# A fused RWKV-7 and SiLU feed-forward kernel: the same 1437 steps in another written order, with other PSUM places

## The chip, the cores and the metric

The kernel runs on one core of one Trainium2 chip. The metric is the device time of one execution in microseconds, from the first to the last instruction and what lies around them; the time before is the median of three runs. TensorE is called PE in the profile (PEld is its weight load), VectorE is DVE, ScalarE is ACT, GpSimd is POOL and SyncE is SP.

## The reference

An RWKV-7 recurrence over 768 tokens for 4 batches and 8 heads of 40 channels, and behind it a feed-forward layer with SiLU on its output, all in float32.

```python
for t in range(S):                                   # S = 768, state is (B, H, D, D), D = 40
    y[:, :, t] = np.einsum('bhd,bhde->bhe', rt, state)
    Sa = np.einsum('bhde,bhe->bhd', state, at)
    state_decay = state * wt[:, :, None, :] - np.einsum('bhd,bhe->bhde', Sa, bt)
    state = state_decay + np.einsum('bhd,bhe->bhde', vt, kt)
...
x = attn_out.transpose(0, 2, 1, 3).reshape(B * S, H * D)   # 3072 x 320
h = x @ w_in                                         # 320 x 2048
g = h * (1.0 / (1.0 + np.exp(-h)))
out = g @ w_out                                      # 2048 x 320
```

## The kernel before

The 768 tokens are cut into 12 chunks of 64 (`NN` = 12). Inside a chunk the recurrence is turned into small matrix products and one triangular inverse per head and batch, 32 of them; from chunk to chunk goes the state `G`. What a chunk does, by the functions that make its steps and the lines that the profile shows for them:

- `load`, `load_r`: SP issues the DMAs of w, b, a, k (512 KB each), v, r and the transposed v.
- `prepare`: DVE makes the running products of w by two scans (`down` L473, `up` L491), scales b and k (`aside`, L510) and a (`scale`, L500). PE multiplies them (`between`, L528, once for b and once for k), DVE masks the k product (L577), PE multiplies it by v (`sv`, L592) and turns k and b (`turn`, L617); ACT copies the results out of PSUM.
- `special` (chunks 0 to 2) and `inverse`/`merge` (the rest, two chunks at a time): the triangular inverse. DVE does it in many small `dots` (L643 multiply, L644 reduce). For chunk 0 PE brings the blocks into place (`spread` L720) and back (`gather` L778). In `special`, `both` (L833), a turn (L846) and three rounds of `more` (L890, added up by DVE in L909) finish it; in `merge`, `first` (L975) and `second` (L1004).
- `chain`: the recurrence from chunk to chunk. PE `right` (L1046, reads `G`), DVE adds it (L1056), PE `solve` (L1070) and `solve_t` (L1101), ACT and DVE copy these out (`vu`, `vut`), PE turns `G` (L1131) and does `update` (L1158), DVE adds to and scales `G` (L1174).
- `read`: PE `look` twice (L1204), DVE masks each (L1216, into `lam`), PE `write_state` (L1243) and `write` (L1258), DVE scales (L1269); the result goes through DRAM into `xt` (`bring`; for chunk 0 straight to `xt`, L1313).
- `moe`: the feed-forward layer of the 256 tokens of the chunk. PE `full` (L1340, 8 matmuls of 128x256) and `rest` (L1353), ACT SiLU (`gate`, L1363), PE `second` (L1380, in pieces of 4 matmuls of 128x320, eight pieces a chunk), then a copy and two stores.
- `weights`: once, the layer's weights come as 64-bit floats through POOL's DMAs and are made into float32 by DVE and ACT (L336 to L354); for three of the ten units PE adds two halves (`sum_`, L360, 128x512) and DVE multiplies (L372).

Every call of `add` makes one step; each step has an engine and a PE shape: `F` is the full 128x128 array (`full`, `second`, `sum_`), `R` 64 rows by 128 columns (`rest`), `H` 128 rows by 64 columns or less (`update`, `write`), `Q` 64x64 quarters (most of the recurrence), `T` the turns, `S` 32x32 (`first`, `second` of `merge`). Nothing sorts the steps when the kernel is built: `Plan.follow` takes them in the order of the numbers in the table `ORDER` and gives each PSUM or `lam` buffer the place that its digit in `SLOTS` names. Each engine carries out its own steps in that order, one after another, and waits at a step for what it reads, for what still reads the place that it writes, and for nothing else. PSUM is four places, `pair0` to `pair3`, of 4 KB in each partition; two `lam` buffers are in SBUF. DMAs stand in the queue of SP, ACT or POOL in the same order, and a DMA that waits holds up those behind it on its queue.

The lines of this that the change works through:

```python
        for room, slot in zip(rooms.values(), slots):
            room.slot, room.tile = int(slot), self.slots[room.kind][int(slot)]
...
        return [self.ops[n] for n in order]
...
        for op in plan.follow([int(n) for n in ORDER.split()], "".join(SLOTS.split())):
            op["do"]()
```

Of the kernel before, what the change touches and what calls it, by code (L numbers as in the profile page):

```python
# [130 lines left out]
"""  # L131

SLOTS = """
02010313103013023201121220321321331102201331232212021000300010012010102103230113332111021202013323111302020230
10211001211003132011132330130003220300213021120013103110133031021231131031100212001201232130132032033001101332
32011022330030001301001320110132012332222001102003101210203231232113030320232121101130100132012
"""
# [1471 lines left out]
```

## Time and profile before

| | |
|---|---|
| median of 3 runs | 690.67 us (689.32 to 693.51) |
| span of the profiled execution, first to last instruction | 690.3 us |
| last matmul ends | 684.3 us |
| DVE busy | 420.9 us, 61% of the span |
| ACT busy | 198.4 us, 29% |
| POOL busy | 13.0 us, 2% |

The profiled execution's own time is its span, and the median of the runs is 0.4 us above it. A matmul in float32 stands in the trace as two records, so that a piece of `second` is 8 records and a `full` 16. Matmul records overlap, since the array is a pipeline; what a step takes on PE is therefore read from its start to the start of the next one and not from its own length. A row of the timeline gives start, length, engine, line, operation and tiles, the number of records, and in brackets the idle time in front with what ended it.

### The profile page before, as it was taken

The page shows a single profiled execution, that of the slowest core. Times are in us where ns is not written, and L with a number is a line of the kernel's source. Part 1 is how long each engine was busy: PE and PEld are TensorE (multiplying, and loading weights), DVE is VectorE, ACT ScalarE, POOL GpSimd, SP SyncE. Part 2 cuts the span into 40 slices and gives each one's busy share as a digit, 9 for nine tenths or more (in the row PEclk, how much of TensorE's full clock was granted, in tenths as well). Part 3 has the DMA queues.
Part 4 walks back from the last instruction along what each step waited for, and adds up shares of the span by engine and source line. Part 5 has one row for each costly group of instructions (what it writes and reads, how often), then busy time and mean ns, then how long its engine had stood idle before and what let it go on. Part 6 is the DMA issues. An engine that isn't in the chain of part 4 may idle for free.

```text
span 690.3 us, 27487 instructions
## 1 busy us (share of the span) xinstructions
PE 656.6 (95%) x12794; PEld 531.4 (77%) x12794; DVE 420.9 (61%) x632; ACT 198.4 (29%) x254; POOL 13.0 (2%) x30
## 2 busy tenths in 40 slices
PE   1589999999999999999999999999999999999996
PEld 1467788788778778878778778778788778788774
DVE  7998988984894558954538962639854773011000
ACT  4562364343214332214222222222223122121020
POOL 3000110000000000000000000000000000000000
PEclk9999999999999999999999999999999999999999
DMA  9945385725255462561730672352542214111100
GB/s 291 296 125 138 92 257 168 183 37 133 78 140 120 103 167 63 128 159 27 194 103 14 193 166 66 104 134 74 152 86 65 74 35 105 28 45 34 42 2 22
DMA packets 113282, 76.64 MB, mean 111 GB/s; under 512 B 61154, under 2 KB 109589, under 8 KB 112520
## 3 DMA queue, kind: packets, MB, share of 16 engines
q1 hardware_dynamic: 110436, 63.71, 36.0%
q0 software_dynamic: 2224, 10.63, 4.7%
q8 instruction: 102, 1.67, 1.0%
q10 hardware_dynamic: 500, 0.46, 0.3%
q14 instruction: 20, 0.16, 0.1%
HBM read 60.03 MB, written 14.35 MB: 108 GB/s over the span
## 4 chain that ended last, share of the span: by engine, by line
PE 87%; DVE 7%; DMA 2%; issue 1%; SPq 1%; ACT 1%; POOL 1%; DVEq 0%; ACTq 0%; POOLq 0%
PE pair L1380 31%; PE pair L1340 24%; PE pair L1353 7%; PE pair L1204 4%; PE pair L528 3%; PE pair L1258 3%; PE pair L1158 2%; PE pair L617 2%; PE pair L1046 2%; PE pair L592 2%; PE pair L1243 2%; PE pair L1070 1%; PE pair L1101 1%; PE pair L890 1%; DVE kbv L473 1%
## 5 line engine op out<-in xcount | busy, mean ns | idle before, releaser
L1380 PE MATMUL pair<-wo,gts 128*128 128x320 f32 x768 | 215.8, 437 | 0.0
L1380 PEld LDWEIGHTS pair<-wo,gts 128*128 128x128 f32 x768 | 143.4, 190 | 58.0 <-issue 1.0
L1340 PE MATMUL pair<-xt,wi 128*128 128x256 f32 x768 | 175.8, 383 | 0.0
L1340 PEld LDWEIGHTS pair<-xt,wi 128*128 128x128 f32 x768 | 143.5, 190 | 22.1 <-issue 0.7
L1363 ACT ACTIVATE gts<-pair 128x1024 f32<-128x1024 f32 x48 | 47.6, 1026 | 91.2 <-PE pair L1353 84.1
L644 DVE TENSOR_REDUCE XI<-XI 128x64 f32<-128x512 f32 (+9 forms) x85 | 58.7, 690 | 2.9
L1216 DVE TENSOR_TENSOR lam<-pair,ml 128x1024 f32<-128x1024 f32 x22 | 26.4, 1220 | 46.6 <-PE pair L1204 29.4
L1353 PE MATMUL pair<-xt,wi 64*128 64x256 f32 x384 | 48.0, 389 | 0.8 <-DMA xt<-X 0.8
L261 DVE COPY ot<-pair 128x320 f32<-128x320 f32 x22 | 10.8, 489 | 57.0 <-PE pair L1380 49.4
L528 PE MATMUL pair<-a,kb 40*64 40x64 f32 x1536 | 30.1, 228 | 15.0 <-DVE a L500 13.4
L1353 PEld LDWEIGHTS pair<-xt,wi 64*128 64x128 f32 x384 | 35.3, 187 | 7.1 <-issue 2.0
L528 PEld LDWEIGHTS pair<-a,kb 40*64 40x64 f32 x1536 | 26.9, 141 | 17.2 <-issue 15.0
L643 DVE TENSOR_TENSOR XI<-XI,mi 128x1024 f32<-128x1024 f32 (+8 forms) x60 | 33.6, 560 | 5.1 <-DMA mi<-md 3.8
L510 DVE TENSOR_TENSOR kb<-kbv 128x512 f32<-128x512 f32 (+1 forms) x36 | 29.9, 862 | 6.6 <-PE pair L528 3.3
L630 ACT COPY kt<-pair 128x640 f32<-128x640 f32 x24 | 16.5, 695 | 56.1 <-PE pair L617 55.9
L1204 PEld LDWEIGHTS pair<-r,vut 40*64 40x64 f32 x1536 | 24.4, 135 | 5.2 <-issue 2.8
L473 DVE TENSOR_TENSOR_SCAN kbv<-wz,zt 128x1024 f32<-128x1024 f32 x12 | 27.5, 2292 | 0.6
L1204 PE MATMUL pair<-r,vut 40*64 40x64 f32 x1536 | 26.8, 220 | 1.0 <-DMA r<-in_rT 0.9
L491 DVE TENSOR_TENSOR_SCAN wz<-wz,zt 128x1024 f32<-128x1024 f32 x12 | 27.5, 2289 | 0.3
L259 ACT ACTIVATE vut<-pair 128x1024 f32<-128x1024 f32 (+1 forms) x13 | 12.5, 958 | 49.4 <-PE pair L1101 45.4
L643 DVE TENSOR_TENSOR XI<-XI,xs 128x1024 f32<-128x1024 f32 (+1 forms) x25 | 25.2, 1008 | 0.6
L937 ACT COPY mi<-XI 128x1024 f32<-128x1024 f32 x5 | 10.0, 2002 | 51.8 <-DVE XI L644 31.7
(160 smaller groups left out, 685.2 us busy)
## 6 DMA issues: line engine op xcount, KB each, us to landing
wz<-in_wT SPq DMA_DIRECT2D x12, 512.0 KB
a<-in_aT SPq DMA_DIRECT2D x12, 512.0 KB
kbv<-in_bT SPq DMA_DIRECT2D x12, 512.0 KB
kbv<-in_kT SPq DMA_DIRECT2D x12, 512.0 KB
vut<-in_vT SPq DMA_DIRECT2D x48, 96.0 KB
r<-in_rT SPq DMA_DIRECT2D x48, 96.0 KB
vu<-in_v SPq DMA_DIRECT2D x24, 160.0 KB
xh<-lam SPq DMA_DIRECT2D x22, 160.0 KB
```

The costliest lines, as they stand in the source:

```text
L473: nc.vector.tensor_tensor_scan(back(V), back(W[:, 2 : 2 + Q * C]), zt, 1.0, ALU.mult, ALU.add)
L491: nc.vector.tensor_tensor_scan(Z, Z, zt, 0.0, ALU.mult, ALU.add)
L510: TTn[engine].tensor_tensor(out=at_(kb, place(is_b, first), (576 * step, 4 // step), (128, 4), (1, C)), in0=blocks((kf, bf)[is_b]), in1=bl ...
L528: nc.tensor.matmul(room.tile[half(b), j, g * C : g * C + C], lhsT=kb[rows(j), place(is_b, q) : place(is_b, q) + C], rhs=A[rows(j), q * C : ...
L643: nc.vector.tensor_tensor(out=at_(tmp, 0, *dims), in0=x, in1=y, op=ALU.mult)
L644: nc.vector.tensor_reduce(out=out_, in_=at_(tmp, 0, *dims), axis=AX.X, op=ALU.add)
L1204: nc.tensor.matmul(pl.tile[half(1 - b if role else b), b, c * C : c * C + C], lhsT=vut[rows(b), role, hu, :], rhs=rs[rows(b), hh, :], star ...
L1216: lambda pl=pl, la=la: nc.vector.tensor_tensor(out=la.tile.rearrange("p (q t) -> p q t", q=Q), in0=pl.tile.rearrange("p a b -> p (a b)").r ...
L1340: nc.tensor.matmul(rooms[g].tile[:, f // 2, (f % 2) * T : (f % 2) * T + T], lhsT=wi[:, k, (4 * g + f) * 128 : (4 * g + f) * 128 + 128], rh ...
L1353: nc.tensor.matmul(rooms[g].tile[:, h, (f % 2) * T : (f % 2) * T + T], lhsT=wi3[half(h), g * 256 + (f % 2) * 128 : g * 256 + (f % 2) * 128 ...
L1363: nc.scalar.activation(out=gts[:, 4 * g * T : 4 * g * T + 4 * T], in_=rooms[g].tile.rearrange("p a b -> p (a b)"), func=AF.Silu)
L1380: nc.tensor.matmul(po[b].tile[:, 0, 0:DM], lhsT=g4[:, f, 128 * b : 128 * b + 128], rhs=wo[:, f, :], start=f == 0, stop=f == NF - 1,)
```

## The change

The change exchanges the two tables `ORDER` and `SLOTS` and nothing else. The same 1437 steps (417 on SP, 394 on DVE, 386 on PE, 223 on ACT, 17 on POOL) stand in another order from the first step on, on every engine, and the buffers have other PSUM and `lam` places. Counted along PE's steps, the shape changes from one to the next 224 times before and 149 times now. Of these, 139 and 64 lie between the full array (`F`) and another shape; the other 85 and 85 lie among the smaller shapes. Up to the first `second` (L1380) PE does the same steps in both orders, but for two that now stand ahead of it, an `sv` of chunk 2 and the `update` of chunk 1; the changes of shape there are 43 before and 40 now, of which 29 and 17 at the full array. From there on they are 181 and 109, of which 110 and 47 at the full array.

```diff
@@ -72,68 +72,68 @@
 ORDER = """
-102 24 0 147 2 114 1 3 4 70 67 6 7 8 9 10 103 14 104 105 15 148 25 106 149 11 115 139 127 150 73 66 75 151 16
...
+24 102 0 1 3 2 70 6 7 9 8 114 127 115 103 104 11 12 13 10 105 106 76 77 78 67 75 74 69 71 5 68 287 64 4 72 14
...
 SLOTS = """
-02010313103013023201121220321321331102201331232212021000300010012010102103230113332111021202013323111302020230
...
+01011322123213010132113203302101221020123002030101100100023213112021212323111122102121120001002203113101021013
...
```

On DVE the first place is the start of the program, behind the `down` scan of chunk 0 (`a_82` is a of chunk 0, `wz_73` and `wz_74` the w of chunks 0 and 1, `kb` the scaled k and b; L336 to L345 belong to the weights):

```order
 L488 MEMSET wz_73 128x16
+L510 TENSOR_TENSOR kb<-kbv 128x2x4x64 x2
 L491 SCALAR_TENSOR_TENSOR wz_73<-wz_73,zt 128x1024
 L492 MEMSET zt 128x16
-L510 TENSOR_TENSOR kb<-kbv 128x2x4x64 x2
+L336 TENSOR_SCALAR wi<-gts 128x2x512
+L510 TENSOR_TENSOR kb<-kbv 128x4x4x64
 L500 TENSOR_TENSOR a_82<-a_82,wz_73 128x1024
-L336 TENSOR_SCALAR wi<-gts 128x2x512
```

The scaling of a, which PE's first step needs, now has one weight step and the scaling of k ahead of it. Behind it, up to the three instructions of L733 that begin the inverse of chunk 0, DVE had ten instructions of weights, masks and the scaling of k; now it has two of the weights (L338, L339) and the whole `down`, `between_` and `up` of chunk 1, which stood behind that inverse before.

On PE at the same place, from the first matmul on, before (`sb_88` is the b product of chunk 0 in SBUF, `XI` holds the blocks of its inverse, `gts` the raw weights):

```order
L528 MATMUL pair_111<-a_82,kb 64x64 x32
L720 MATMUL pair_112<-ident,sb_88 64x64 x32
L528 MATMUL pair_113<-a_82,kb 64x64 x32
L617 MATMUL pair_114<-ident,kb 128x40 x16
L617 MATMUL pair_111<-ident,kb 128x40 x16
L360 MATMUL pair_113<-gts,ident 128x512
L778 MATMUL pair_114<-ident,XI 64x64 x32
```

and now:

```order
L528 MATMUL pair_111<-a_82,kb 64x64 x32
L617 MATMUL pair_112<-ident,kb 128x40 x16
L720 MATMUL pair_113<-ident,sb_88 64x64 x32
L617 MATMUL pair_114<-ident,kb 128x40 x16
L360 MATMUL pair_111<-gts,ident 128x512 x3
L528 MATMUL pair_112<-a_82,kb 64x64 x32
L360 MATMUL pair_111<-gts,ident 128x512
L778 MATMUL pair_113<-ident,XI 64x64 x32
```

Three more weight sums stand ahead of `gather` (L778), and one turn ahead of `spread` (L720).

In the middle of the program, PE in chunk 2's `chain` and `read`, from `solve_t` (L1101) on, before:

```order
L1101 MATMUL pair_113<-X_93,R_92 40x64 x32
L1380 MATMUL pair_111<-wo,gts 128x320 x4
L1204 MATMUL pair_113<-r,vut 64x64 x32
L592 MATMUL pair_112<-vu_99,lam_116 64x40 x32
L1380 MATMUL pair_111<-wo,gts 128x320 x4
L1204 MATMUL pair_112<-r,vut 64x64 x32
L1243 MATMUL pair_113<-r,GT 40x64 x32
L1380 MATMUL pair_111<-wo,gts 128x320 x4
L617 MATMUL pair_114<-ident,kb 128x40 x16
```

and now:

```order
L1101 MATMUL pair_113<-X_93,R_92 40x64 x32
L592 MATMUL pair_112<-vu_99,lam_116 64x40 x32
L1070 MATMUL pair_111<-R_92,X_93 64x40 x32
L1204 MATMUL pair_113<-r,vut 64x64 x32
L1204 MATMUL pair_112<-r,vut 64x64 x32
L1243 MATMUL pair_111<-r,GT 40x64 x32
L1158 MATMUL pair_113<-vu_98,kt_87 40x40 x32
L1258 MATMUL pair_111<-lam_116,kt_87 40x64 x16
L1258 MATMUL pair_111<-lam_115,kt_87 40x64 x16
L617 MATMUL pair_112<-ident,kb 128x40 x16
L1380 MATMUL pair_114<-wo,gts 128x320 x16
```

The pieces of `second` that stood between the small steps now follow as one block of 16 matmuls (four pieces). The same is done in most chunks. Between the second `look` and `write` there was a piece of `second` or a `full` before in most chunks; now there are `write_state` and `update`, or `first` and `update`.

DVE's order at this place of chunk 9, now: the two masks of `look` (L1216) directly one behind the other, the state's sum behind them (`vu_99` is that chunk's v and u):

```order
L263 TENSOR_SCALAR vu_99<-pair_111 64x2x4x80
L1216 TENSOR_TENSOR lam_115<-pair_113,ml 128x1024
L1216 TENSOR_TENSOR lam_116<-pair_114,ml 128x1024
L1174 TENSOR_TENSOR G<-pair_113,G 128x2x8x40
L261 COPY ZQ<-pair_111 32x512
L1174 TENSOR_TENSOR G<-G,wc_108 128x2x8x40
L1269 TENSOR_TENSOR lam_115<-pair_112,wz_73 128x4x4x64
```

What moved there is work of the inverse (L643, L644), of which before some stood ahead of the masks and more between the masks and the sum; now it starts behind these rows.

On SP, w, b, k, a of chunk 0 is now the order of the first four loads (w, a, b, k before). On POOL, the fetch of the last unit of `w_in` went from the second to the sixth place, and POOL's four of the DMAs that bring chunk 0's result into `xt` (L1313) stand ahead of all fetches of `w_out` but one. The last step of all is now the count of the finite checks (L1448 to L1459), whose matmul ran at 549.6 us before.

More of the change, by code (lines that the diff above doesn't have):

```diff
@@ L74 @@
 ORDER = """
[56 rows of a table removed]
[56 rows of a table added]
 """
 SLOTS = """
-02010313103013023201121220321321331102201331232212021000300010012010102103230113332111021202013323111302020230
-10211001211003132011132330130003220300213021120013103110133031021231131031100212001201232130132032033001101332
-32011022330030001301001320110132012332222001102003101210203231232113030320232121101130100132012
+01011322123213010132113203302101221020123002030101100100023213112021212323111122102121120001002203113101021013
+01302021033120123011331300011303032122211212203212312000130232321031100212210310003323331103131011100031202031
+20301020121121001301021033021103222302323120101230303111330203022112010120101323201021302301230
 """
```

110 rows, old and new, of the table ORDER are left out of this document.

## The prediction

> **What bounds the kernel now.** I read the page first, then PE's waits, then the span in stretches.
>
> ```profile
> span 690.3 us, 27487 instructions
> PE 656.6 (95%) x12794; PEld 531.4 (77%) x12794; DVE 420.9 (61%) x632; ACT 198.4 (29%) x254; POOL 13.0 (2%) x30
> ```
>
> Two answers follow: who PE waited for (in total, times, longest), and busy time by stretch (us, PE, PEld, DVE, ACT, POOL, granted clock, DMA share, GB/s).
>
> ```profile
> PE pair L528 <- DVE a L500: 13.4, 1, 13.4
> PE pair L778 <- ACT XI L773: 6.7, 1, 6.7
> ```
>
> ```profile
> 0.00:13.30 13.30, 0.00 (x0) 0.00 (x0) 10.24 (x32) 5.14 (x5) 6.62 (x19) 1.00 0.87 300
> 0.00:117.00 117.00, 90.10 (x2248) 73.58 (x2248) 103.56 (x172) 54.17 (x65) 11.87 (x28) 0.97 0.66 193
> 33.50:60.00 26.50, 24.03 (x604) 18.53 (x604) 24.90 (x37) 12.70 (x17) 0.57 (x1) 0.94 0.50 137
> 117.00:684.40 567.40, 566.52 (x10548) 457.77 (x10546) 317.38 (x461) 143.85 (x190) 1.12 (x2) 1.00 0.37 95
> ```
>
> There are two kernels in one. From 117 us, where the first L1380 starts, PE works 566.5 of 567.4 us: what it does there, it pays in full, and nothing else counts as long as it is never kept waiting. Before 117 us PE is idle 26.9 us (117.0 less 90.1), 13.4 of them ahead of its first matmul and 13.5 in waits, while DVE works 103.6: that part is a chain through DVE with PE in it. The change touches both, so the sum has a term for each.
>
> **Term 1, the changes of shape.** The same instructions cost PE more or less by what stands beside them. Start times say it best (rows of the timeline: start, length, operation, records).
>
> ```profile
> 605.04 3.62 PE L1340 MATMUL pair<-xt,wi 128*128 128x256 f32 x16
> 608.49 2.32 PE L1380 MATMUL pair<-wo,gts 128*128 128x320 f32 x8
> 610.64 3.62 PE L1340 MATMUL pair<-xt,wi 128*128 128x256 f32 x16
> 614.19 1.10 PE L1101 MATMUL pair<-X,R 64*40 64x64 f32 x64
> ```
>
> ```profile
> 173.57 1.16 PE L1204 MATMUL pair<-r,vut 40*64 40x64 f32 x64
> 174.55 1.09 PE L592 MATMUL pair<-vu,lam 64*64 64x40 f32 x64
> 175.57 2.42 PE L1380 MATMUL pair<-wo,gts 128*128 128x320 f32 x8
> 177.92 1.16 PE L1204 MATMUL pair<-r,vut 40*64 40x64 f32 x64
> ```
>
> Between two full-array steps an L1380 takes 610.64 - 608.49 = 2.15 us; between two small ones 177.92 - 175.57 = 2.35. So 0.10 for each of its two boundaries. A full L1340 takes 3.45 ahead of another full step and 614.19 - 610.64 = 3.55 ahead of a small one: 0.10 again. The small neighbour pays too: L1204 took 0.98 ahead of L592, and L592 took 1.02 ahead of L1380, while the L592 at 301.26 (quoted below) took 0.95 ahead of a small step: 0.07. A stay in the full array so costs 0.20 on its own side and about 0.07 on the side of the step before it, 0.27 for two boundaries, or 0.14 each. Bounds: 0.10 if the small side saves nothing, 0.20 if it pays as much as the full side at both of its ends.
>
> The order has 75 boundaries of the full array fewer (139 to 64); the changes among the smaller shapes stay 85. 75 x 0.14 = 10.5 us, bounds 7.5 and 15.0; I take the value that is measured on both sides. 63 of them lie behind the first L1380, where PE is the bound, so they count in full; the other 12 are in PE's part of the start. The Trainium skill says in TensorEngine Tiling (Array Packing), Key Properties, that a change of the tiling mode, not of the tile alone, drains the array. By that rule every change of shape would cost, so that only the 75 fewer of 224 are saved, which is what the rows give too; the page has no price, and the rows have one.
>
> **Term 2, the start.** The chain of chunk 0 in DVE's and PE's rows:
>
> ```profile
> 12.09 1.22 DVE L500 TENSOR_TENSOR a<-a,wz 128x1024 f32<-128x1024 f32 x1
> 13.22 0.69 DVE L336 TENSOR_SCALAR wi<-gts 128x1024 int32<-128x1024 int32 x1
> 24.52 1.51 DVE L733 SCALAR_TENSOR_TENSOR xs<-pair,dm,xs 128x256 f32<-128x256 f32 x3
> 32.23 0.23 DVE L471 TENSOR_SCALAR w<-wz,pad 128x16 f32<-128x16 f32 x1
> 38.24 1.20 DVE L791 TENSOR_TENSOR mi<-pair,dm 128x1024 f32<-128x1024 f32 x1
> ```
>
> ```profile
> 13.41 1.99 PE L528 MATMUL pair<-a,kb 40*64 40x64 f32 x64 [13.41 <-DVE a L500]
> 16.68 3.65 PE L720 MATMUL pair<-ident,sb 64*64 64x64 f32 x61 [1.29 <-ACT sb L259]
> 24.72 2.07 PE L360 MATMUL pair<-gts,ident 128*128 128x512 f32 x2
> 33.50 3.75 PE L778 MATMUL pair<-ident,XI 64*64 64x64 f32 x64 [6.71 <-ACT XI L773]
> 37.18 1.17 PE L360 MATMUL pair<-gts,ident 128*128 128x512 f32 x2
> ```
>
> The first matmul waits for L500, and now one L336 (0.7) and the second L510 (as large as L500, which took 13.22 - 12.09 = 1.13 to the next start) stand ahead of it: 13.4 + 1.8 = 15.2. The loads should be there: with a, the fourth on SP now, 2 MB have come there, beside 1 or 2 MB of weights on POOL, and the first 13.3 us moved 300 GB/s, 4 MB. That is just in time, and a late by 1 us is the bound above.
>
> L720 started 3.27 behind the first matmul. From 15.2, it can start at 18.5 and end at 22.1, and ACT's copy of it takes 0.5: 22.6. DVE comes to L733 behind L338 and L339 (1.1 and 0.6, as L500 and L336) and the scans of chunk 1, which took 38.24 - 32.23 = 6.0: a's scaling ends at 15.2, so at 22.9. L733 starts at 22.9 instead of 24.5, and `gather` (L778) is asked for at 33.5 - 1.6 = 31.9. Behind it the scans no longer hold up L791.
>
> PE has three more weight sums and one L528 ahead of `gather`. The sums wait for ACT's two conversions of the raw weights:
>
> ```profile
> 21.64 0.47 ACT L750 ACTIVATE xs<-pair,dm 128x256 f32<-128x256 f32 x1
> 23.04 1.22 ACT L340 ACTIVATE gts<-gts 128x1024 f32<-128x1024 int32 x1
> 24.12 0.70 ACT L630 COPY kt<-pair 128x640 f32<-128x640 f32 x1
> 24.70 1.16 ACT L354 ACTIVATE gts<-gts 128x1024 f32<-128x1024 uint32 x1
> ```
>
> Behind L750 at 22.6 come L630 and these two, 0.6 + 1.1 + 1.1, so the first sum at 25.3, some 2.5 us after PE's last turn. Four sums of 1.1 (37.18's kind) and an L528 of 1.0 fill PE to 30.7, and `gather` waits 1.2 instead of 6.7. At half speed (24.72's sum took 2.07) they end at 35.6 and `gather` is 2.1 us late instead of 1.6 early. Waits now: 0.4 ahead of L720 (18.5 less 15.2, the matmul's 2.0 and a turn of 0.9), 2.5, 1.2, and of the others (13.5 less 6.7 ahead of L778 and the 1.3 between 15.4 and L720's 16.68, so 5.5) I keep 2, since those behind `gather` hang on L791, which the scans held up: 6.1 in place of 13.5. So +1.8 and -7.4: -5.6. Bounds: 0 (the waits fall by 1.8 alone) and -9 (the 2 and part of the 2.5 vanish).
>
> DVE doesn't forbid it. Before, its last step for the first L1380, the weights' product, was
>
> ```profile
> 105.47 1.22 DVE L352 TENSOR_TENSOR wo<-wo,raw 128x1024 f32<-128x1024 f32 x1
> ```
>
> done at 106.7, 10.4 us ahead of PE. Now four instructions more stand ahead of it, one of L336's size and three of L500's, 4.3 us: 111.0 with all its old idle time. PE comes at 117.1 - 5.6 + 2.3 (the two steps more) - 1.7 (12 boundaries of Term 1): 112.1.
>
> The stretch from 33.5 to 60 shows the granted clock at 0.94, and the sum at 24.72 ran at half the speed of the one at 37.18. The Trainium skill (TensorE: Matmul & The Clock Gate, What's actually happening) has half the clock by default and after an idle window of about 3.4 us: by it the sums ahead of `gather` start at half speed, and the start saves up to 3.7 us less (35.6 for 31.9). The rows agree that it was slow there, but not for how long PE must work first: 24.72 comes after 8 us of nearly unbroken matmuls.
>
> **Term 3, new waits behind 117 us.** Small steps now follow each other without a `second` between them, so their copies must fit under less.
>
> ```profile
> L1216 DVE TENSOR_TENSOR lam<-pair,ml 128x1024 f32<-128x1024 f32 x22 | 26.4, 1220 | 46.6 <-PE pair L1204 29.4 <-issue 9.5 <-ACT kt L630 7.6
> ```
>
> ```profile
> 281.42 1.40 PE L1158 MATMUL pair<-vu,kt 128*40 128x40 f32 x64
> 282.74 1.16 PE L528 MATMUL pair<-a,kb 40*64 40x64 f32 x64
> ...
> 301.26 1.14 PE L592 MATMUL pair<-vu,lam 64*64 64x40 f32 x64
> 302.21 1.12 PE L1046 MATMUL pair<-G,a 40*64 40x40 f32 x64
> 303.26 0.75 PE L975 MATMUL pair<-ZQ,sb 32*32 32x32 f32 x64
> 303.95 3.72 PE L1340 MATMUL pair<-xt,wi 128*128 128x256 f32 x16
> ```
>
> Between the second `look` and `write` stand `first` (303.95 - 303.26 = 0.69) and `update` (1.32), 2.0 us, or `write_state` and `update`, 2.3. Under them one mask of 1.22 must end, begun about 0.2 late behind the first mask: 1.4 us. It fits with 0.6 to spare, because the masks stand next to each other. Before, all waits behind 117 us were 0.9 together (567.4 less 566.5); I take 1.2 more, 0.1 in each of eleven chunks, with bounds 0 and 6 (0.5 in each).
>
> The rest costs nothing: POOL's fetch of the last `w_in` unit, moved behind four others, is needed by the fourth L1340 alone, just ahead of the first L1380; of SP's queue the four loads of chunk 0 stay first; `xt` of chunk 0 goes ahead of the fetches of `w_out` on POOL, and the check's matmul at the end runs beside the last copy and store, which end the span.
>
> **Sum.** 690.3 - 10.5 - 5.6 + 1.2 = 675.4 on the profile's own span; the median is 0.4 above it: 675.8.
>
> **The rivals.** *The start gives nothing* (waits move, clock low): 690.7 - 10.5 + 1.2 = 681.4. For it: the half-speed sums, and `gather`'s chain with every later step behind it. Against it: DVE ends L352 10 us before PE needs it, so there is room.
>
> *A new wait in every chunk, and slower.* If the three instructions from L471 to the scan behind it, or another 2.3 us of DVE's work (a scan is near half of the 6.0 above), get between `look`'s product and its mask, `write` waits 2.3 + 1.4 - 2.0 = 1.7 us, and `right` behind the state's sum once more, some 3 us a chunk in eleven chunks: 690.7 - 16.1 + 33 = 708. It takes the gain away at 14.9 / 11 = 1.4 us a chunk and is slower by 1% from 2.0. Against it stands DVE's order at that place, masks next to each other.
>
> *The boundary's price belongs to the step and not to the change* (what a stay saves at its edge comes back inside the longer run, as waits for the PSUM places that a run needs at once): 690.7 - 5.6 + 1.2 = 686.3, within 1%. Against it: runs of L1380 inside the full array are 2.15 in every row of that kind.
>
> **How the numbers follow.** One per cent, about what a measurement of this kernel can tell from no change, is 6.9 us: faster means below 683.8. The forecast has 0.72; the start that gives nothing 0.15; the price that comes back 0.08; the wait in every chunk 0.05. Faster 0.87, same 0.08, slower 0.05. Below, Term 1 at 15.0 or the start at -9 take off 4.5 or 3.4, and both hardly come together: 668. Above, the start at 0 gives the first rival's 681.4, and 1.6 more of Term 3 on it 683. What lies outside is the 0.13 of the last two rivals and some 0.05 below: 668 to 683.
>
> **What would show it.** After its start PE is busy all but a microsecond or two from the first L1380 on; an L1380 takes 2.15 inside its run and no row of 2.35 but at single pieces; the first matmul is at 15.2, `gather` near 32, the first L1380 between 107 and 114. Wrong it is if PE's waits list names L1216, L1174 or L1363 with more than 5 us together, or if the first L1380 is behind 117.

## The result: 12.7% slower, and the profile after

The changed kernel takes 780.37 us (775.76 to 782.41, four runs), the one before 690.56 beside it: a ratio of 1.127, interval 1.122 to 1.132. The forecast was 675.8. Ratios here and below leave out executions more than 1.5% above the fastest of the same kernel, where the granted clock is lower too.

The profile's first lines, its instruction queue (packets, MB, share of 16 DMA engines), and two stretches, to the first L1380 and from there to the last matmul:

```profile
span 779.6 us, 27470 instructions
PE 692.2 (89%) x12794; PEld 574.0 (74%) x12794; DVE 422.0 (54%) x632; ACT 197.3 (25%) x254; POOL 12.5 (2%) x30
...
q8 instruction: 102, 1.67, 0.9%
```

```profile
0.00:132.50 132.50, 90.76 (x2376) 76.11 (x2376) 99.83 (x164) 54.77 (x67) 11.36 (x28) 0.94 0.59 171
132.60:772.60 640.00, 601.38 (x10426) 497.82 (x10418) 321.93 (x467) 142.12 (x188) 1.12 (x2) 0.92 0.32 84
```

The same 12794 matmuls now keep PE busy 692.2 us instead of 656.6. On the profiled spans (779.6 against 690.3) the 89.3 us divide so: the first L1380 starts at 132.6 instead of 117.1, 15.5 us; from there to the end of the last matmul 640.0 instead of 567.2, 72.8; behind it 1.0. In that middle part PE is idle 640.0 - 601.4 = 38.6 us (0.9 before) and busy 34.9 us longer, though it has fewer boundaries; the granted clock is 0.92 there and was 1.00. The records of the clock show two values only, full and half, and 99 us of the 640 at half.

PE's waits in the middle part (total, times, longest):

```profile
PE pair L592 <- issue: 8.3, 4, 2.8
PE pair L1204 <- issue: 7.8, 6, 1.8
PE pair L1243 <- issue: 5.1, 4, 2.0
PE pair L528 <- issue: 4.1, 3, 1.5
PE pair L1070 <- issue: 4.0, 4, 1.4
...
PE pair L1204 <- DMA mi<-md: 1.5, 1, 1.5
```

Hardly anything is waited for: "issue" is time in which the engine waited for nothing that the profile shows. With the rows left out it comes to 36.0 us, all of it ahead of small steps. No mask and no state sum is in the list; two copies of ACT's and the SiLU (L1363) are, with 1.0 us together. Where it happens, in chunk 4 behind a run of eight L1380:

```profile
278.67 1.14 PE L1046 MATMUL pair<-G,a 40*64 40x40 f32 x64
279.62 1.70 PE L528 MATMUL pair<-a,kb 40*64 40x64 f32 x99
282.82 1.00 PE L528 MATMUL pair<-a,kb 40*64 40x64 f32 x27 [1.50 <-issue]
283.54 0.32 PE L1101 MATMUL pair<-X,R 64*40 64x64 f32 x2
...
288.35 0.77 PE L1204 MATMUL pair<-r,vut 40*64 40x64 f32 x32
290.64 1.56 PE L1204 MATMUL pair<-r,vut 40*64 40x64 f32 x91 [1.52 <-DMA mi<-md]
...
292.05 0.66 PE L1243 MATMUL pair<-r,GT 40*40 40x64 f32 x33
294.09 1.09 PE L1243 MATMUL pair<-r,GT 40*40 40x64 f32 x30 [1.38 <-issue]
295.11 2.36 PE L1158 MATMUL pair<-vu,kt 128*40 128x40 f32 x64
297.26 3.23 PE L1258 MATMUL pair<-lam,kt 128*40 128x64 f32 x64
300.43 0.92 PE L1340 MATMUL pair<-xt,wi 128*128 128x256 f32 x3
```

The gaps stand in the middle of steps, not at their starts, where a step would wait for its operands. L1158 and L1258 behind the last gap take 297.26 - 295.11 = 2.15 and 3.17 us; L1158 took 1.32 before. The records of the clock have it at half from 293.1 to 299.9.

What the gaps have in common comes out of the trace by counting. Number PE's instructions (matmuls, weight loads and PE's own waits on semaphores) from the start, and set the packets of the instruction queue beside them, each 1.67 MB / 102 = 16.4 KB:

```
gap ends   gap    PE's instruction,   the last packet of the
(us)       (us)   modulo 256          instruction queue ended
242.48     2.84   194                 1.64 us earlier
282.82     1.50   193                 1.34
290.64     1.52   194                 0.91
294.09     1.38   194                 1.34
353.49     2.73   194                 1.37
397.43     1.79   193                 1.50
401.15     1.61   193                 1.34
```

Of the 29 gaps above 0.35 us behind 117 us, 28 end at instruction 193 or 194 modulo 256, 0.9 to 1.6 us behind the end of an instruction packet. So PE gets its instructions 256 at a time and had come to the end of what was there; the gap at 290.64 is one of them too, put down to a DMA by the rule that the last event is to blame. The number 193 itself says nothing, since the trace doesn't show what PE ran ahead of its first recorded instruction; that it is the same each time does. No two packets start less than 3.41 us apart in this trace, and 3.10 in that of before. A small step is 128 such instructions in 0.95 us, two of them use a packet up in 1.9; an L1380 is 16 instructions in 2.15. The Trainium skill has the size (Advanced Engine Details and Errata, ISA Cache: lines of 256 instructions, and only two of them, though it gives TensorE four times the memory of the others); the trace agrees by the count of 256, and the blocks below, which stall after 332 to 524 instructions, fit two lines. How long a line takes to come that section doesn't say.

### The profile page after: what moved, and what is told of

Its sections match the earlier page's. It is cut to its first block, busy times and chain, and to the rows that moved or that the text cites. A ratio compares the mean times of both kernels' runs of the same rounds, so it can differ in the third digit from the quotient of the medians.

```text
span 779.6 us, 27470 instructions
## 1 busy us (share of the span) xinstructions
PE 692.2 (89%) x12794; PEld 574.0 (74%) x12794; DVE 422.0 (54%) x632; ACT 197.3 (25%) x254; POOL 12.5 (2%) x30
## 3 DMA queue, kind: packets, MB, share of 16 engines
q8 instruction: 102, 1.67, 0.9%
## 4 chain that ended last, share of the span: by engine, by line
PE 85%; issue 6%; DMA 5%; DVE 2%; SPq 1%; ACT 1%; DVEq 0%; ACTq 0%
PE pair L1380 27%; PE pair L1340 22%; PE pair L1353 6%; PE pair L1204 4%; PE pair L1258 4%; DMA wz<-in_wT 3%; PE pair L528 3%; PE pair L1158 3%; PE pair L890 2%; PE pair L1243 2%; PE pair L1101 2%; PE pair L592 2%; PE pair L1070 2%; PE pair L617 2%; PE pair L1046 2%
## 5 line engine op out<-in xcount | busy, mean ns | idle before, releaser
L1380 PE MATMUL pair<-wo,gts 128*128 128x320 f32 x768 | 215.3, 440 | 0.0
L1380 PEld LDWEIGHTS pair<-wo,gts 128*128 128x128 f32 x768 | 146.6, 193 | 61.3 <-issue 3.4
L1340 PE MATMUL pair<-xt,wi 128*128 128x256 f32 x768 | 170.7, 381 | 0.0
L1340 PEld LDWEIGHTS pair<-xt,wi 128*128 128x128 f32 x768 | 145.4, 190 | 21.3
L1363 ACT ACTIVATE gts<-pair 128x1024 f32<-128x1024 f32 x48 | 47.1, 1024 | 201.6 <-PE pair L1353 201.4
L644 DVE TENSOR_REDUCE XI<-XI 128x64 f32<-128x512 f32 (+9 forms) x85 | 58.7, 690 | 2.9
L528 PE MATMUL pair<-a,kb 40*64 40x64 f32 x1536 | 32.2, 231 | 29.4 <-DVE a L500 22.9
L528 PEld LDWEIGHTS pair<-a,kb 40*64 40x64 f32 x1536 | 28.5, 144 | 31.6 <-issue 31.1
L1204 PE MATMUL pair<-r,vut 40*64 40x64 f32 x1536 | 36.6, 257 | 11.9 <-issue 10.4
L1353 PE MATMUL pair<-xt,wi 64*128 64x256 f32 x384 | 46.3, 386 | 0.0
L1216 DVE TENSOR_TENSOR lam<-pair,ml 128x1024 f32<-128x1024 f32 x22 | 26.6, 1222 | 32.4 <-PE pair L1204 31.0
L1204 PEld LDWEIGHTS pair<-r,vut 40*64 40x64 f32 x1536 | 33.9, 169 | 13.6 <-issue 11.9
L643 DVE TENSOR_TENSOR XI<-XI,mi 128x1024 f32<-128x1024 f32 (+8 forms) x60 | 33.7, 562 | 10.8 <-DMA mi<-md 9.2
L263 DVE TENSOR_SCALAR vu<-pair 64x640 f32<-64x640 f32 x9 | 7.3, 817 | 50.8 <-ACT vu L259 50.8
L1258 PE MATMUL pair<-lam,kt 128*40 128x64 f32 x704 | 29.5, 259 | 0.2 <-issue 0.2
L1258 PEld LDWEIGHTS pair<-lam,kt 128*40 128x40 f32 x704 | 28.0, 149 | 1.1 <-issue 1.0
L1269 DVE TENSOR_TENSOR lam<-pair,wz 128x1024 f32<-128x1024 f32 x11 | 13.5, 1223 | 23.3 <-PE pair L1258 23.3
```

The source lines that it names most:

```text
L528: nc.tensor.matmul(room.tile[half(b), j, g * C : g * C + C], lhsT=kb[rows(j), place(is_b, q) : place(is_b, q) + C], rhs=A[rows(j), q * C : ...
L643: nc.vector.tensor_tensor(out=at_(tmp, 0, *dims), in0=x, in1=y, op=ALU.mult)
L644: nc.vector.tensor_reduce(out=out_, in_=at_(tmp, 0, *dims), axis=AX.X, op=ALU.add)
L1204: nc.tensor.matmul(pl.tile[half(1 - b if role else b), b, c * C : c * C + C], lhsT=vut[rows(b), role, hu, :], rhs=rs[rows(b), hh, :], star ...
L1258: nc.tensor.matmul(py.tile[rows(j), b, c * C : c * C + C], lhsT=K[:, q, j], rhs=lam[m].tile[:, l * C : l * C + C], start=fresh(py, b, j), ...
L1340: nc.tensor.matmul(rooms[g].tile[:, f // 2, (f % 2) * T : (f % 2) * T + T], lhsT=wi[:, k, (4 * g + f) * 128 : (4 * g + f) * 128 + 128], rh ...
```

## The experiments

**The two halves.** One kernel has the changed order up to its first L1380 and the rest in the order of before, one the reverse; PSUM places follow in a few buffers. Of ORDER's rows in the first:

```diff
-102 24 0 147 2 114 1 3 4 70 67 6 7 8 9 10 103 14 104 105 15 148 25 106 149 11 115 139 127 150 73 66 75 151 16
+24 102 0 1 3 2 70 6 7 9 8 114 127 115 103 104 11 12 13 10 105 106 76 77 78 67 75 74 69 71 5 68 287 64 4 72 14
...
```

> The changed order up to its first L1380, then the rest of the steps in the order of before, with PSUM places to suit. Theory S (supply): PE's instructions come in packets of 256 on the instruction queue, no packet sooner than about 3.5 us after the last; small steps use one up in 1.9 us, and only pieces of the full array between them give the queue time. Theory C (clock): unbroken small tiles alone bring the granted clock down, and the gaps only follow. By both the loss lies in the order behind the first L1380: here it is gone and only the later start is left, first L1380 near 132, time 690.6 + 15.5 = 706 (702 to 710), no wait of PE on issue over 2 us in total behind it. Rival P: the later start (late loads and a late weight fetch) or DVE's new order in it is what spoils the middle: then 760 to 780.

> The order of before up to its first L1380, then the rest in the changed order. Theories S and C: the start of before comes back, first L1380 near 117 to 122, and the loss behind it stays: 780.4 - 15.5 = 765 (760 to 770), with 30 us or more of PE's waits on issue and 90 us or more at half the granted clock. Rival P: 690 to 700.

Measured: 728.29 us (ratio 1.050, interval 1.044 to 1.055) and 777.25. From the first L1380 to the end, first kernel, then second:

```profile
152.70:721.10 568.40, 567.31 (x10418) 457.37 (x10418) 310.70 (x455) 138.05 (x182) 1.12 (x2) 0.99 0.35 90
```

```profile
126.70:768.70 642.00, 596.74 (x10422) 492.93 (x10418) 314.29 (x455) 139.56 (x185) 1.12 (x2) 0.93 0.31 80
```

568.4 and 642.0 us, where before and after have 567.2 and 640.0; PE's waits on issue there are 0.8 and 43.2 us, and the clock is at half for 5.9 and 89.2. The loss of the middle lies in the order there, whatever start it has, and rival P falls. The totals missed what was expected (706 and 765), since each joint has waits of its own that neither kernel has: the first L1380 is at 152.7 and 126.7, and in the first kernel PE waits 16.4 us ahead of an L528 for ACT (L522) and 9.4 ahead of that L1380 for ACT (L604). One of four executions of the second took 765.2 and the others, the profiled one among them, 776.9 to 778.4, so it has no ratio; 765.2 too is 73 us above before.

**PSUM places.** The order of before with other places for 140 of its 315 buffers:

```diff
-02010313103013023201121220321321331102201331232212021000300010012010102103230113332111021202013323111302020230
+02010313103013023201121220321321331102201331232202021000300010012011102103231113332122120111023313202301010130
...
```

> The kernel before, its order untouched, with other PSUM and lam places for 140 of its 315 buffers (always the place that has been free the longest). If the new places are part of the loss: slower by over 1%. If not: 690 to 692, as before.

691.11 us, ratio 0.999, interval 0.998 to 1.001 (one of ten executions, which the ratio leaves out, took 845.6): other places cost nothing by themselves. These are not the changed kernel's own places, which can't be had without its order.

**Small steps by themselves.** Three kernels are the one before with work on PE behind its last matmul. From the first of them (the other two leave out the `range(2)` in their small steps):

```diff
             op["do"]()
+        quarters = [
+            (b, role, 8 * j + 2 * z + x, 4 * j + 2 * z + x)
+            for j in range(2) for z in range(2) for x in range(2) for role in range(2) for b in range(2)
+        ]
...
+        def dense(p):
+            for _ in range(2):
+                for b, role, q, c in quarters:
+                    nc.tensor.matmul(pairs[p][half(1 - b if role else b), b, c * C : c * C + C], lhsT=vut[rows(b), role, q, :], rhs=rs[rows(b), q, :], start=True, stop=True)
...
+        run(0, 8)
+        for i in range(20):
+            dense(1 + i % 3)
+        run(0, 8)
```

> The kernel before with extra work on PE behind its last matmul, whose results nobody reads: (dense) 20 steps of 32 matmuls of 40x64 by 64 columns like look's, unbroken; (wide) 10 steps with the same quarter tiles by 256 columns; (mixed) 12 times two small steps and a full-array piece of 4 matmuls; (halved) the same with a piece of 2; (spaced) 12 times a full-array piece of 3 matmuls that waits for an ACT copy of the one before. Between them 8 pieces of the full array, 17 us. S: dense has gaps at every 256th instruction and takes 10 packets x 3.5 = 35 us in place of 20 x 0.96 = 19; wide, with a quarter of the instructions per us, has no gap and the full clock, 38 us; mixed none, 12 x 4.3 = 51; halved 0.4 us a packet, 12 x 3.6 = 43 to 46 in place of 38; spaced, without small tiles, shows whether idle gaps of over 1 us bring the clock down by themselves. C: wide and mixed show the half clock as dense does (wide 60 us and more), and spaced keeps the full clock.

`quarters` has 32 entries, so that the `range(2)` made each small unit of this run twice what the expectation says: dense is 40 steps of look's size and 20 packets, mixed and halved have four steps ahead of a piece. Dense, wide and spaced, and then dense in two parts, parted at 707:

```profile
701.17:772.06 70.89, 68.31 (x2562) 66.36 (x2561) 0.00 (x0) 0.00 (x0) 0.00 (x0) 0.54 0.02 4
...
791.04:860.27 69.23, 69.23 (x1281) 48.87 (x1281) 0.00 (x0) 0.00 (x0) 0.00 (x0) 1.00 0.01 2
...
1108.75:1143.92 35.17, 22.32 (x73) 12.77 (x72) 0.00 (x0) 11.26 (x11) 0.00 (x0) 1.00 0.00 0
```

```profile
701.17:707.00 5.83, 4.64 (x299) 4.51 (x302) 0.00 (x0) 0.00 (x0) 0.00 (x0) 1.00 0.01 3
707.00:772.06 65.06, 63.67 (x2276) 61.85 (x2267) 0.00 (x0) 0.00 (x0) 0.00 (x0) 0.50 0.02 5
```

Dense takes 70.89 / 20 = 3.54 us a packet, with hardly any other DMA at work (share 0.02), so contention isn't what makes packets late. After 5.8 us the clock is at half and stays there: at half clock two steps take as long as a packet, and hardly a gap is left to see. So the 3.54 alone can't tell the supply from the clock; the next run does. Wide has the same tiles and half the instructions in the same time: clock 1.00, no gap. Small tiles alone don't bring the clock down, and theory C falls in that form; a long row of 64-column steps whose packets come in time is in no run. Mixed and halved, with four steps ahead of each piece, take 8.39 and 7.89 us a round, where the supply at 3.5 us a packet would give 7.2 and 7.1: their packets were late by up to 1.6 and 1.9 us, and 17.1 and 35.2 us ran at half clock. Spaced, with PE busy 63% of the time and gaps of 1.2 us, keeps the full clock.

> Again the kernel before with work on PE behind its last matmul, unread. (1) 12 times two small steps and a full piece of 4 matmuls, 272 PE instructions in 4.25 us; (2) the same with a piece of 2, 264 in 3.2; (3) 20 small steps, unbroken, with 128 columns instead of 64, 128 instructions in 1.75 us each; (4) 12 times a full-array piece of 2 matmuls and a wait for two ACT copies, PE busy 1.1 of about 3.4 us; (5) 12 times one small step and the same wait, 128 instructions in 3.4 us, PE busy 1.0 of it. S: 256 instructions need 3.54 us (the dense run took 70.9 us for 20 packets), so (1) has no issue gap and (3) none or gaps under 0.2, (2) 0.3 to 0.7 in each; (4) and (5) have none. Whether the clock falls through low work alone: then (4) and (5) show the half clock though no packet is late; if it falls only with late packets, they keep the full clock, as the run spaced did with PE busy 60% of the time.

Its five parts in order, and the fourth until its clock falls:

```profile
701.95:754.37 52.42, 52.42 (x1634) 40.93 (x1634) 0.00 (x0) 0.00 (x0) 0.00 (x0) 1.00 0.01 4
771.68:815.21 43.53, 42.35 (x1586) 33.64 (x1585) 0.00 (x0) 0.00 (x0) 0.00 (x0) 1.00 0.02 5
832.53:867.62 35.09, 35.09 (x1281) 34.92 (x1280) 0.00 (x0) 0.00 (x0) 0.00 (x0) 1.00 0.02 5
884.95:936.80 51.85, 27.39 (x49) 13.31 (x48) 0.00 (x0) 22.53 (x22) 0.00 (x0) 0.55 0.00 0
954.93:1002.48 47.55, 22.48 (x769) 20.34 (x768) 0.00 (x0) 22.54 (x22) 0.00 (x0) 0.54 0.01 2
```

```profile
884.95:890.60 5.65, 2.59 (x9) 1.25 (x7) 0.00 (x0) 2.84 (x3) 0.00 (x0) 1.00 0.00 0
```

(1) is 52.42 / 12 = 4.37 us a round and has room. (2) should take 3.2 and takes 3.63 at the full clock, which is 3.52 for 256 instructions (3.58 from the third round on, which starts at 778.31): that is the supply. Little of it shows as a gap (1.2 us in all); the small steps are drawn out instead. (3) runs just at the supply and loses nothing. (4) and (5) have no late packet, yet the clock falls, in (4) after PE had worked 2.59 of 5.65 us. So little work alone brings the clock down, and a packet that takes 3.5 us for 1.9 us of work (54%) comes near that. In dense the packets were late while the clock was still full: by that order the half clock follows from late packets and doesn't make them late.

> The kernel before with unread work on PE behind its last matmul: blocks of 2, 3, 4, 5, 6, 8, 10 and 12 small steps (look's shape, 128 PE instructions and 0.96 us each), twice through, with 6 full-array pieces (13 us) between blocks. S, with one packet of 256 fetched ahead at most, whatever the length of the run before: blocks of 2 and 3 take 0.96 a step; from the fourth or fifth step on each further step costs 1.77 (half of 3.54), so that a block of 6 takes 6.5 to 8 instead of 5.8, and one of 12 some 17 to 19 instead of 11.5, in part at half clock. If a long run of the full array filled a deep store instead, blocks of 6 and more would be free too.

The blocks of the first pass, 2 to 12 steps:

```profile
701.12:703.15 2.03, 2.03 (x130) 1.96 (x129) 0.00 (x0) 0.00 (x0) 0.00 (x0) 1.00 0.00 0
716.26:719.22 2.96, 2.96 (x193) 2.89 (x192) 0.00 (x0) 0.00 (x0) 0.00 (x0) 1.00 0.03 6
732.34:737.66 5.32, 4.21 (x257) 4.00 (x256) 0.00 (x0) 0.00 (x0) 0.00 (x0) 1.00 0.01 3
750.78:759.68 8.90, 5.81 (x321) 5.42 (x320) 0.00 (x0) 0.00 (x0) 0.00 (x0) 0.88 0.01 4
775.07:785.34 10.27, 7.32 (x385) 6.93 (x384) 0.00 (x0) 0.00 (x0) 0.00 (x0) 0.81 0.02 5
799.85:811.63 11.78, 9.49 (x513) 9.10 (x513) 0.00 (x0) 0.00 (x0) 0.00 (x0) 0.87 0.02 4
826.64:843.85 17.21, 14.56 (x642) 14.12 (x641) 0.00 (x0) 0.00 (x0) 0.00 (x0) 0.67 0.02 5
858.12:880.00 21.88, 19.14 (x770) 18.14 (x769) 0.00 (x0) 0.00 (x0) 0.00 (x0) 0.62 0.02 4
```

Three steps are free (0.93 for the third), the fourth costs 2.4 us, and twelve take 21.9 instead of 11.4. But three is where these blocks happen to stand in the count: counted in the trace, the first gap comes after 428, 332, 364, 524, 428 and 332 instructions in the blocks of 4, 5, 6, 8, 10 and 12 steps, so between 2.6 and 4.1 steps are free, and the gap ends at the same number modulo 256 as above. The run of 13 us ahead stores no more than that. The blocks of 6 and 12 take 2 to 3 us more than the ranges expected; the second pass, which stands at the same places in the count, gives 7.75, 9.88, 12.35, 17.06 and 22.01 from five steps on.

**The pieces put back.** The changed kernel with PE's steps alone in another order, all other engines in the changed one. PE in chunk 3:

```diff
 L592 MATMUL pair_114<-vu_98,lam_116 64x40 x32
-L1101 MATMUL pair_111<-X_94,R_90 40x64 x32
 L1070 MATMUL pair_112<-R_90,X_94 64x40 x32
-L1243 MATMUL pair_113<-r,GT 40x64 x32
-L1204 MATMUL pair_114<-r,vut 64x64 x32
-L1204 MATMUL pair_111<-r,vut 64x64 x32
+L1380 MATMUL pair_111<-wo,gts 128x320 x4
+L1101 MATMUL pair_113<-X_94,R_90 40x64 x32
+L1204 MATMUL pair_114<-r,vut 64x64 x32
+L1204 MATMUL pair_113<-r,vut 64x64 x32
+L1380 MATMUL pair_111<-wo,gts 128x320 x4
 L975 MATMUL pair_112<-ZQ,sb_88 32x32 x32
```

> The changed kernel with PE's steps alone in another order behind the first L1380: full-array pieces stand between the small steps again, so that 134 boundaries of the full array are left in place of 64 (139 before); SP, DVE, ACT and POOL keep the changed order step for step, and PSUM places follow. S (supply): the waits on issue behind the first L1380 fall from over 38 us to 5 to 10, the half clock nearly goes, the boundaries cost about 9 us again: 780.4 - 83 + 9 + some 5 to 15 of new waits for the other engines, whose order was not made for this = 710 to 722. P (what spoils the middle is the changed order of DVE and ACT, or their copies): 760 or more, with PE waiting for DVE or ACT.

> Like the run with the pieces put back (the changed kernel, PE's steps alone in another order behind the first L1380, all other engines in the changed order step for step), but with the small steps laid so that every 256th instruction of PE, counted with its waits on semaphores and the turns at half the count of a small step, is reached no sooner than its packet can be there: asked for some 300 instructions ahead, 3.8 us on the way, 3.5 us apart. 136 boundaries of the full array, 134 in that run. S in this form: the part behind the first L1380 takes 579 by the model where it gave 591 for that run (598 measured), so 580 to 588, waits on issue under 5 us, no or one window of half clock; time 710 to 724 where that run had 736.8. If that run lost its time to the changed order of DVE and ACT, or to something else that a stretch of small steps brings, this one stays at 730 to 740.

From the first L1380 to the end, in the one and the other:

```profile
127.70:725.70 598.00, 577.04 (x10425) 461.99 (x10418) 320.30 (x462) 141.78 (x187) 1.12 (x2) 0.99 0.34 89
```

```profile
124.70:718.40 593.70, 577.51 (x10422) 462.68 (x10418) 320.25 (x464) 141.50 (x187) 1.12 (x2) 0.99 0.35 90
```

736.76 us (ratio 1.067, 1.063 to 1.071) and 726.92 (1.048, 1.045 to 1.052). More boundaries of the full array, 134 and 136 for 64, and the kernel is 44 and 53 us faster than the changed one; the middle fell from 640.0 to 598.0 and 593.7. So 42.0 and 46.3 of the 72.8 us come back by moving PE's steps alone. Both missed their ranges, by 15 and 3 us. The 30.8 and 26.5 us that are left hold late packets (15.5 of 21.0 us idle in the first, 6.2 of 16.2 in the second, the rest being waits for DVE, ACT and loads) and 13.7 and 17.1 us at half clock; how much of them is the other engines' changed order is not shown. Between the two, only where the steps fall against the packets was meant to differ: PE waits 9.3 us less on issue and some 4.5 more for the others, and the middle is 4.3 us shorter. The rest of the 10 us between them isn't shown to be the packets'.

**Before, laid anew.** PE's steps of the kernel before in three other orders, each from a model of prices and packets; rows as in the diff above.

> The kernel before with PE's steps in another order behind the first L1380, found with a model of the steps' prices and of one packet of 256 instructions per 3.6 us; other engines keep before's order. 141 boundaries of the full array, longest stretch of small steps 736 instructions (832 before). S: the few waits of PE behind the first L1380 shrink, 686 to 689 where before has 690 to 692 (-0.5%). Rival: those waits are the other engines' and move on with it: no difference.

> As the first reordering of PE's steps in the order of before, with the packet model corrected by what that run showed (a packet is asked for 290 to 400 instructions ahead and is there 4.4 us later, with 0.3 us to spare): 143 boundaries of the full array. The model gives 1 to 3 us less than before, so 688 to 692, no difference that counts; the first one came out at 699.9 because packets were late at two places (1.4 and 1.0 us, the first with a window of half clock behind it) and a DMA wait had come. If lateness of packets isn't what made that one slow, this one is at 695 to 702 as well.

> The kernel before with PE's steps in another order behind the first L1380, laid by the same count of instructions; the two runs of this kind before it (699.9 and 712.8) had counted the turns double and left the waits out, so that their packets' ends lay elsewhere than thought. The model gives 3.3 us less than before (682.4 against 685.7), most of it from waits of PE on DVE's work, and 1.0 us of late packets: 686 to 690, no more than 0.7% under before. If it is over 695 again, the count isn't what failed there.

699.87 us (1.013, 1.011 to 1.016), 712.83 (1.032, 1.029 to 1.035), 693.02 (1.001, 1.000 to 1.003). All three missed. With 141, 143 and 143 boundaries in place of 139, two lost 8 and 22 us, with packets late in a few places, the half clock behind some of them and a wait of 2.4 and 3.1 us for a load of v; the third, with the instructions counted better, lost nothing and won nothing. No version that beats the kernel before was found.

**a of chunk 0 as the second load.**

```diff
-24 102 0 1 3 2 70 6 7 9 8 114 127 115 103 104 11 12 13 10 105 106 76 77 78 67 75 74 69 71 5 68 287 64 4 72 14
+24 102 0 2 1 3 70 6 7 9 8 114 127 115 103 104 11 12 13 10 105 106 76 77 78 67 75 74 69 71 5 68 287 64 4 72 14
```

> The changed kernel with one DMA moved: a of chunk 0 goes from the fourth to the second place on SP, as before. Theory: DVE's wait of 7.5 us for a goes, first matmul at 14 to 15 in place of 22.9; the next wait of DVE, 4.7 us on the w of chunk 1, comes forward and grows, so that gather (L778) and the first L1380 gain less: 3 to 8 us, time 772 to 777. Rival: chunk 1's w lands at 29.3 whatever is ahead of it and all of the gain is waited away there: 780. Other rival: what is late is all of SP's queue, because POOL's fetches take the bandwidth, and the first matmul stays behind 20.

776.11 us (1.123, 1.118 to 1.128), the expected size, but its executions (773.58 to 780.44) overlap those of the changed kernel, and the expected reason isn't there: the first matmul came at 17.6, since DVE now waited for k, whose scaling stands ahead of a's. DVE's waits on loads, in the changed kernel and here:

```profile
DVE a L500 <- DMA a<-in_aT: 7.5, 1, 7.5
DVE w L471 <- DMA wz<-in_wT: 4.7, 1, 4.7
```

```profile
DVE w L471 <- DMA wz<-in_wT: 4.4, 1, 4.4
DVE kb L510 <- DMA kbv<-in_kT: 2.3, 1, 2.3
```

Three other runs with the changed start, a as the fourth load, had the first matmul at 16.3 to 17.0 and waited 1.0 to 1.6 us for a, but each 4.7 to 4.9 for the w of chunk 1. So the 22.9 of the profile is partly that execution's, and a's place on the queue isn't shown to matter; the wait for chunk 1's w comes back in every run.

## Why the prediction was wrong

**Term 1 had its price right.** A run of eight L1380 in the changed kernel takes (338.42 - 321.09) / 8 = 2.17 each:

```profile
321.09 17.49 PE L1380 MATMUL pair<-wo,gts 128*128 128x320 f32 x64
338.42 7.07 PE L1340 MATMUL pair<-xt,wi 128*128 128x256 f32 x32
```

The price can be had by itself now: a round of two small steps and a piece takes 4.37, its parts 2 x 0.94 and 2.15, so a stay costs 0.34 and a boundary 0.17 (0.14 taken, 0.10 to 0.20 given). By that price 75 boundaries fewer save some 13 us; no run shows the saving by itself, since what came with it is several times as large.

**The step that failed is Term 3**, the new waits behind 117 us: its 1.2 us and the bound of 6 above all. It asked of each longer stretch of small steps whether the copies of other engines fit under it, and never whether PE's own instructions do; the sentence ahead of it, that nothing else counts as long as PE "is never kept waiting", took PE's supply for granted. So did the description of the kernel, by which an engine waits for operands and places "and for nothing else". The longest row of small steps behind the first L1380, counted in the traces, is 736 PE instructions before and 2336 now. A small step's 0.95 us was read where a piece of the full array stood near, and taken to hold in such rows too; in a block of twelve a step takes 1.8. The masks were in fact no problem. In place of +1.2 the middle lost 72.8 us and Term 1's saving behind the first L1380: 38.6 idle, the rest in steps that take longer, most of it at half clock (PE works 92.0 of those 99 us, which at the full clock would be some 46, an estimate by halving). How much of the second part the clock adds to what the supply takes anyway is open, since at half clock a step is just as slow as its packets.

**Term 2 was wrong in sign.** First matmul 15.2 forecast, 16.3 to 17.0 in three runs and 22.9 in the profile: the bound of 1 us for a was too small. The larger fault is chunk 1's w: the scans were moved ahead of L733 with no look at when their load is there, and L733 came at 35.3 instead of 22.9 (28.8 to 29.7 in the three other runs):

```profile
29.33 0.24 DVE L471 TENSOR_SCALAR w<-wz,pad 128x16 f32<-128x16 f32 x1 [4.69 <-DMA wz<-in_wT]
...
35.34 0.47 DVE L733 SCALAR_TENSOR_TENSOR xs<-pair,dm,xs 128x256 f32<-128x256 f32 x1
```

The first L1380 was forecast at 112.1 and is at 132.6; the two kernels with the pieces put back, which have the same order up to there, reach it at 127.7 and 124.7, so part of the 132.6 is that execution's. Late packets have a part in that too: between 44.4 and 132.6 PE waits 9.8 us on issue, 1.0 in the like stretch before.

**The rivals.** The one on the slower side had a wait in every chunk, by DVE between look and mask, and 708; waits came in most chunks, by another mechanism. The start gave less than nothing. The price that comes back has the 2.17 of the long run against it. The clock was weighed for the start alone, as a matter of warming up. The Trainium skill (TensorE: Matmul & The Clock Gate, What's actually happening) has it fall after an idle window of about 3.4 us; here it fell with no idle stretch above 2.2 us in part (4), so that rule, read as a window without any work, is too narrow for this trace.

**What would show it** did in part: the signs named as wrong were L1216, L1174 and L1363 in the waits, of which only L1363 is there, with 0.3 us, and the first L1380 behind 117, which is.

## What to carry to other kernels

Count PE's instructions, not only its time: 256 of them need some 3.5 us to come, and what is there ahead lasted for 332 to 524 instructions, which is 2.6 to 4.1 float32 steps of 32 small matmuls (128 instructions in 0.95 us each), by where the row begins in the count. What looks like a costly change of shape between them, a piece of the full array with 16 instructions in 2.15 us, is the time in which the next ones come. Before pulling like work together, look at what its neighbours were giving it.

## What the runs showed of the hardware

- Under steady demand 256 instructions came every 3.5 to 3.6 us in part (2), at the full clock and with a DMA share of 0.02, though a packet's transfer on the queue lasts 1.1 (the median of 102 in the changed kernel). So most of that time isn't the transfer.
- The clock's records change in steps of 3.41 us. With full-array matmuls and gaps it stayed full at 63% busy and fell at 46%. In dense PE was shown busy for 2.23 of the last 3.41 us before the fall, and spaced held the full clock with 1.89 in such a stretch (1116.58 to 1119.99); dense then stayed at half for 65 us with PE busy all but 1.4 of them. So the busy time of the profile alone doesn't tell when the clock falls.
- With the same order of loads, DVE's wait for a was 1.0, 1.1, 1.6 and 7.5 us in four profiles.
